# Three chained layers on one core: layer 1's products over token blocks of 512 and 256 instead of 384

## The chip, the cores and the metric

The kernel runs on one core of a Trainium2 chip. The metric is the device time of one execution in microseconds. Time before: median 847.4 us of 3 runs (847.13 to 849.57). TensorE is written PE, VectorE DVE, ScalarE ACT, GpSimd POOL; SP is the engine from whose queue all DMAs are issued.

## The reference

Local attention over q, k, v of shape (4, 8, 576, 64) in chunks of 64 tokens gives 2304 tokens of 512 values. Then two layers with a hidden width of 2048:

```python
x = attention(q, k, v)              # (2304, 512), softmax inside chunks of 64
h = x @ w_in1                       # layer 1, up
x = (h * tanh(log1p(exp(h)))) @ w_out1   # layer 1, down
h = x @ w_in2                       # layer 2, up
g = where(h >= 1, h, where(h <= -1, 0, (h + 1) ** 2 / 4))
out = g @ w_out2                    # layer 2, down, (2304, 512) float32
```

The weights arrive as 64-bit floats, two 32-bit words each.

## The kernel before, in words

Every matrix product is done in three passes of a reduced-precision float format (fp32r): an operand is split into a high and a low half, and high x high, high x low and low x high are added up in PSUM. The weights are loaded as words, put together into 32-bit floats by ACT, POOL and DVE, and split (w_part: the high half is `hi`, a copy on ACT or DVE, the low half `lo` at L345, a subtraction on POOL or DVE).

Stage 1 is attention, 18 tiles of 128 tokens, and layer 1's up product. attention() loads q, k, v, transposes on PE (L505), makes scores (L521), exponentiates on ACT (L542), normalises, transposes again (L565), multiplies with v (L577) and writes the two halves of its part of x (the second at L592). Three tiles fill one x block of 384 tokens; two x blocks are in memory at a time. up() multiplies one x block with one of 16 slices of w_in1: 12 matmuls of 384 columns into one of four banks of the set B (L606), called a step here. ACT applies Mish from the bank into a z buffer (L853); two steps share a buffer of 384 KB, and z_store sends it to DRAM (L616). There are two such buffers. Attention uses the four banks of the set A.

Stage 2 is layer 1's down product. g_pair loads 384 KB of z back (L631), ACT makes the high half and DVE the low half (L636); down() adds 12 matmuls of 384 columns of each slice into four banks (L653), one per 128 output columns, over 16 slices. The blocks alternate between the bank sets A and B. At a block's end the banks are copied (ACT or DVE) and stored to DRAM (L873).

Stage 3, layer 2's up product, multiplies sevenfold: seven products of smaller matrices take the place of eight, so x and the weights are first added and subtracted. x_seven loads one of three groups of 768 tokens (L441), makes sums with DVE (L386) and splits them (L380 and a copy), into seven pieces `x2` per group. w_seven does the same to the weights and stores them to DRAM (L406); w_back loads them (L409). seven() does one unit: one group with one weight slice, 42 matmuls of 384 columns (L780), in four banks of A or B in turn. Stage 4, layer 2's down product, works likewise with 256 columns (L723).

The order of instructions on each engine is set ahead by a planner (class Plan). Each operation has an engine, an assumed duration, a due time (prio) and perhaps an earliest time (release); the planner lets time run and picks, on each engine, the ready operation with the least due time. The chip then works through each engine's fixed list, waiting with semaphores. Buffers without a ring have fixed places in one memory of 154 KB per partition (PLACES); an operation on one waits until everything that lay there has been read. Fixed rings are listed in FIXED: "z" has two places of 3072 bytes, "z2" six.

Before the first up product, PE is given filler matmuls (L942) in its idle time; they end with the second up step.

Of the kernel before, what the change touches and what calls it, by code (L numbers as in the profile page):

```python
# [8 lines left out]
F32 = mybir.dt.float32  # L9
F32R = mybir.dt.float32r  # L10
# [154 lines left out]
def kernel(  # L165
# [28 lines left out]
    NBLK = NT // NB  # L194
    scale = 1.0 / float(D) ** 0.5
# [8 lines left out]
    spill = [dp.tile([P, 2 * NB], F32, name=f"z{b}") for b in range(NBLK * NF // 2)]  # L204
# [3 lines left out]
    x2d = [dp.tile([P, KD * NB], F32, name=f"x{b}") for b in range(NBLK)]  # L208
# [225 lines left out]
    def x_seven(q, tau, after=()):  # L434
# [3 lines left out]
        for d, t in ((0, 0), (0, 1), (1, 1), (1, 0)):  # L438
            x = xs[d, t] = ("xh", q, d, t)
            new(x, "ld" if q == 2 else "z" if d == 0 else "z2", [P, 2, NB])  # L440
            dma(384, lambda _, x=x, d=d, t=t: nc.sync.dma_start(  # L441
                out=get(x).rearrange("p m t -> p (m t)"), in_=x2d[2 * q + t][:, 2 * d * NB:2 * (d + 1) * NB]
            ), reads=[("x2d", 2 * q + t, m) for m in (2 * d, 2 * d + 1)] + list(after), writes=[x], tiles=[x], prio=tau)
# [32 lines left out]
    def attention(i, tau, release=0.0):  # L476
# [81 lines left out]
        op(*(("DVE", 0.69) if i < TB else (("DVE", "POOL"), (0.69, 1.6))), norm, reads=[("ri", i)], writes=[e], tiles=[e], **kw)  # L558
# [26 lines left out]
        x, o = ("x", i // TB), i % TB * P  # L585
        if o == 0:
            new(x, None, [P, 2, KD, NB], F32R)
# [9 lines left out]
    def up(n, x, b, j, xkeys, tau, tag):  # L597
        h, w = ("h", n, b, j), ("w", n, j)
        new(h, tag, [P, 512])

        def products(_):
            wt, xt, ps = get(w), get(x), get(h)[:, 0:NB]
# [8 lines left out]
        op("PE", 2.09, products, reads=[*xkeys, (w, 0), (w, 1)], writes=[h], tiles=[h, w, x], prio=tau)  # L611
        return h

    def z_store(n, b, jp, tau):
        z = ("z", n, b, jp)
        dma(384, lambda _: nc.sync.dma_start(  # L616
            out=spill[b * NF // 2 + jp].rearrange("p (j t) -> p j t", j=2) if n == 0 else
            spill2[jp].rearrange("p (j t) -> p j t", j=2)[:, :, b * NB:(b + 1) * NB], in_=get(z)
        ), reads=[(z, 0), (z, 1)], writes=[("spill", n, b, jp)], tiles=[z], prio=tau)

    pairs = []

    def g_pair(b, jp, tau):

        zl, g = ("zl", b, jp), ("g", 0, b, jp)
        new(zl, "z2", [P, 2, NB])
        new(g, None, [P, 2, 2, NB], F32R)

        after = pairs[-3:-2]
        pairs.append((g, 0))  # L630
        dma(384, lambda _: nc.sync.dma_start(  # L631
            out=get(zl).rearrange("p j t -> p (j t)"), in_=spill[b * NF // 2 + jp]
        ), reads=[("spill", 0, b, jp), *after], writes=[zl], tiles=[zl], prio=tau, release=tau - 20)
        op("ACT", 0.86, lambda e: copy(e, get(g)[:, 0], get(zl)),
           reads=[zl], writes=[(g, 0)], tiles=[zl, g], prio=tau)
        op("DVE", 0.98, lambda _: nc.vector.tensor_tensor(  # L636
# [3 lines left out]
    def down(b, j, tau):  # L640
        w, g, a = ("w", 1, j), ("g", 0, b, j // 2), j % 2
# [5 lines left out]
        def products(_):  # L647
            wt, gt = get(w), get(g)
            gh, gl = gt[:, 0, a], gt[:, 1, a]
            for m, y in enumerate(ys):  # L650
                wh, wl = (wt[:, x, m * P:(m + 1) * P] for x in range(2))
                for x, (l, r) in enumerate(((wh, gh), (wh, gl), (wl, gh))):
                    nc.tensor.matmul(  # L653
                        out=get(y)[:, 0:NB], lhsT=l, rhs=r, start=(j == 0 and x == 0), stop=(j == NF - 1 and x == 2)
# [320 lines left out]
```

## Time and profile before

| | |
|---|---|
| median of the runs | 847.4 us |
| span of the profiled execution | 846.0 us (the runs lie 1.1 to 3.6 us above it) |
| PE busy | 833.0 us, 98% |
| DVE, ACT, POOL busy | 613.1, 422.9, 94.8 us |
| first up step, first down step, first step of layer 2 | 37.09, 279.57, 479.25 us |
| DMA | 205.55 MB, mean 243 GB/s |

Times in rows are microseconds from the span's start. Matmuls are pipelined: a row's duration runs to the modelled end of its last matmul, so the pace is read from starts.

### The profile page before, as it was taken

The numbers are of one execution on the slowest core, as the hardware profiler recorded it, in microseconds if no ns is written. First come the engines' busy times: TensorE is split into PE (matmuls) and PEld (weight loads), VectorE is DVE, ScalarE is ACT, GpSimd is POOL, SyncE is SP. The second block draws the span as 40 slices with busy tenths as digits, with TensorE's granted clock in tenths as the row PEclk, the third lists the DMA queues.
The fourth block names the chain that finished last, engine by engine and source line by source line (L and its number), as shares of the span: only waits on it lengthen the run. The fifth ranks groups of instructions, "written<-read, shape, count | busy, mean of one in ns | idle before, by whom it ended". The sixth has DMA issues, their size and how long they took to land.

```text
span 846.0 us, 16274 instructions
## 1 busy us (share of the span) xinstructions
PE 833.0 (98%) x6358; PEld 817.8 (97%) x6358; DVE 613.1 (72%) x1062; ACT 422.9 (50%) x656; POOL 94.8 (11%) x104
## 2 busy tenths in 40 slices
PE   9999999999999999999999999999999899999997
PEld 8899999999999999999999999999999899999997
DVE  4898867587735768588657788666777679878883
ACT  3574646566634434355434566555566434333341
POOL 1464212133301010000000000000000000000000
PEclk9999999999999999999999999999999999999999
DMA  8869675899779989988898936655679965444431
GB/s 197 212 207 266 193 212 163 247 279 276 210 246 363 327 317 353 364 330 279 308 362 300 355 150 214 243 193 194 239 247 405 401 216 161 127 136 134 142 101 50
DMA packets 145581, 205.55 MB, mean 243 GB/s; under 512 B 63840, under 2 KB 114016, under 8 KB 141408
## 3 DMA queue, kind: packets, MB, share of 16 engines
q1 hardware_dynamic: 145504, 204.51, 72.1%
q8 instruction: 50, 0.82, 0.4%
q14 instruction: 27, 0.22, 0.1%
HBM read 123.73 MB, written 80.74 MB: 242 GB/s over the span
## 4 chain that ended last, share of the span: by engine, by line
PE 86%; DMA 7%; DVE 4%; ACT 2%; issue 1%; POOL 0%; SPq 0%; DVEq 0%; ACTq 0%; POOLq 0%
PE B L606 18%; PE A L653 12%; PE B L653 12%; PE A L723 11%; PE A L780 10%; PE B L723 10%; PE B L780 9%; DMA memory<-in_moe_w_in_dram 3%; PE A L505 2%; PE B L942 2%; DMA zz<-memory 1%; DMA memory_r<-v 1%; PE A L521 1%; PE A L577 1%; DMA memory<-in_moe_w_out_dram 1%
## 5 line engine op out<-in xcount | busy, mean ns | idle before, releaser
L275 ACT ACTIVATE memory_r<-memory 128x768 fp32r<-128x768 f32 (+3 forms) x206 | 163.6, 827 | 204.9 <-PE A L653 28.8
L606 PE MATMUL B<-memory_r 128*128 128x384 f32 x1152 | 213.8, 339 | 1.1 <-POOL memory_r L345 0.8
L606 PEld LDWEIGHTS B<-memory_r 128*128 128x128 f32 x1152 | 197.6, 188 | 4.2 <-POOL memory_r L345 1.3
L723 PE MATMUL A<-memory_r 128*128 128x256 f32 x840 | 104.0, 283 | 2.1 <-DVE memory_r L699 1.1
L723 PEld LDWEIGHTS A<-memory_r 128*128 128x128 f32 x840 | 102.1, 192 | 2.9 <-DVE memory_r L699 1.6
L653 PE MATMUL A<-memory_r 128*128 128x384 f32 x576 | 101.6, 334 | 0.0
L653 PE MATMUL B<-memory_r 128*128 128x384 f32 x576 | 101.6, 334 | 0.0
L653 PEld LDWEIGHTS A<-memory_r 128*128 128x128 f32 x576 | 100.0, 188 | 0.0
L653 PEld LDWEIGHTS B<-memory_r 128*128 128x128 f32 x576 | 100.0, 188 | 0.0
L780 PE MATMUL A<-memory_r 128*128 128x384 f32 x504 | 91.6, 335 | 1.3 <-ACT memory L275 0.7
L780 PE MATMUL B<-memory_r 128*128 128x384 f32 x504 | 90.7, 334 | 0.0
L780 PEld LDWEIGHTS A<-memory_r 128*128 128x128 f32 x504 | 87.5, 188 | 2.8 <-ACT memory L275 1.4
L699 DVE TENSOR_TENSOR memory_r<-memory,memory_r 128x768 fp32r<-128x768 f32 (+1 forms) x72 | 76.9, 1087 | 15.6 <-ACT memory_r L275 15.0
L780 PEld LDWEIGHTS B<-memory_r 128*128 128x128 f32 x504 | 87.5, 188 | 0.2 <-DMA memory_r<-v 0.2
L723 PE MATMUL B<-memory_r 128*128 128x256 f32 x672 | 82.8, 283 | 0.0
L316 POOL TENSOR_SCALAR memory<-memory 128x512 f32<-128x512 f32 x64 | 49.5, 775 | 290.2 <-ACT memory L313 288.0
L723 PEld LDWEIGHTS B<-memory_r 128*128 128x128 f32 x672 | 81.6, 192 | 0.0
L636 DVE TENSOR_TENSOR memory_r<-memory,memory_r 128x768 fp32r<-128x768 f32 x48 | 46.0, 962 | 45.9 <-ACT memory_r L275 42.8
L853 ACT ACTIVATE memory<-B 128x384 f32<-128x384 f32 x96 | 44.9, 489 | 47.9 <-PE B L606 38.2
L380 DVE TENSOR_TENSOR memory_r<-memory,memory_r 128x768 fp32r<-128x768 f32 (+3 forms) x69 | 56.2, 829 | 8.2 <-ACT memory_r L275 8.0
L685 DVE TENSOR_TENSOR memory<-memory 128x256 f32<-128x256 f32 (+1 forms) x108 | 52.3, 508 | 7.7 <-DMA memory<-zz 6.8
L275 ACT ACTIVATE memory<-A 128x512 f32<-128x512 f32 (+2 forms) x58 | 30.5, 541 | 50.4 <-PE A L505 21.1
(54 smaller groups left out, 812.6 us busy)
## 6 DMA issues: line engine op xcount, KB each, us to landing
z<-memory SPq DMA_DIRECT2D x48, 384.0 KB, 3.6
memory<-z SPq DMA_DIRECT2D x48, 384.0 KB, 6.3
zz<-memory SPq DMA_DIRECT2D x48, 384.0 KB, 4.2
memory<-zz SPq DMA_DIRECT2D x72, 256.0 KB, 3.3
memory<-in_moe_w_in_dram SPq DMA_DIRECT2D x32, 512.0 KB, 5.5
memory<-in_moe_w_out_dram SPq DMA_DIRECT2D x32, 512.0 KB, 6.3
v<-memory_r SPq DMA_DIRECT2D x16, 1024.0 KB, 7.9
memory_r<-v SPq DMA_DIRECT2D x16, 1024.0 KB, 9.2
```

The costliest lines, as they stand in the source:

```text
L275: nc.scalar.activation(out=out, in_=in_, func=AF.Copy)
L316: nc.gpsimd.tensor_scalar(out=get(dec), in0=get(dec), scalar1=HIGH, scalar2=-HIGH, op0=ALU.min, op1=ALU.max)
L380: nc.vector.tensor_tensor(out=out(1), in0=in_(), in1=out(0).bitcast(F32), op=ALU.subtract)
L505: nc.tensor.transpose(out=get(ps)[:, p, :], in_=get(qk)[:, x, 2 * p:2 * p + 2, :].rearrange("t h d -> t (h d)"), identity=ident,)
L606: nc.tensor.matmul(out=ps, lhsT=a, rhs=xt[:, r, kk, :], start=(kk == 0 and y == 0), stop=(kk == KD - 1 and y == 2),)
L636: op("DVE", 0.98, lambda _: nc.vector.tensor_tensor(out=get(g)[:, 1], in0=get(zl), in1=get(g)[:, 0].bitcast(F32), op=ALU.subtract), reads= ...
L653: nc.tensor.matmul(out=get(y)[:, 0:NB], lhsT=l, rhs=r, start=(j == 0 and x == 0), stop=(j == NF - 1 and x == 2))
L685: op("DVE", length, lambda _: nc.vector.tensor_tensor(out=out(), in0=a(), in1=b(), op=ALU.subtract), reads=reads, writes=writes, tiles=[zl ...
L699: op("DVE", length, lambda _, a=a, b=b, x=x, c=c: nc.vector.tensor_tensor(out=get(g)[:, :, 1, a:b], in0=get(x)[:, :, c:], in1=get(g)[:, :, ...
L723: nc.tensor.matmul(out=get(ys[bank])[:, half], lhsT=gt[:, l, c], rhs=wt[:, a, r], start=(jp == 0 and half == 0 and y == 0), stop=(jp == NF ...
L780: nc.tensor.matmul(out=ps, lhsT=l, rhs=xt[:, r, kk, :], start=(first and kk == 0 and y == 0), stop=(kk == 1 and y == 2), skip_group_check= ...
L853: op("ACT", 0.5, lambda _, h=h, z=z, j=j: nc.scalar.activation(out=get(z)[:, j % 2], in_=get(h)[:, 0:NB], func=AF.Mish), reads=[h], writes ...
```

## The change

Layer 1's tokens are cut into blocks of 512, which fill a PSUM bank, and one of 256: for the up product the 256 come first (UP: tiles 0 and 1; then four tiles each), for the down product last (DOWNS). The number of blocks is five instead of six. Mish's result of one step is now one z buffer (512 x 4 bytes per partition), stored by itself into a DRAM tensor per slice; g_load brings one slice of one block instead of two slices. The rings keep their sizes. x blocks now lie at 138 and 122 KB, g at 14 to 38 KB in six places, the last two slices of w_out1 at 38 and 62 KB, the x2 groups one third further on (group 0 at 42 to 84 KB, where slices 0 to 4 and 15 of w_out1 lie), w7s at 122 and 0 KB, and the planner's durations and due times follow the widths. Up's blocks have 4 attention tiles, spaced over the block before. x2d, layer 1's output in DRAM, is one tensor per half.

```diff
+    WIDE = 512
+    UP = [(0, NT % WIDE)] + [(NT % WIDE + i * WIDE, WIDE) for i in range(NT // WIDE)]
+    DOWNS = [(i * WIDE, WIDE) for i in range(NT // WIDE)] + [(NT - NT % WIDE, NT % WIDE)]
+    TILES = [range(t // P, (t + n) // P) for t, n in UP]
+    OF = {i: b for b, r in enumerate(TILES) for i in r}
...
-    ORDER = (4, 1, 0, 3, 5, 6, 2)
+    ORDER = (4, 1, 0, 2, 5, 6, 3)
...
-        "w": lambda n, j: KB * ((4 * j, 66 + 4 * j if j < 15 else 60)[n]),
-        "x": lambda b: KB * (130 + 12 * (b % 2)),
-        "g": lambda n, b, jp: KB * (42 + 6 * ((b * NF // 2 + jp) % 3)),
-        "g7": lambda u: KB * (28, 126, 140)[u % 3],
-        "x2": lambda q, c: KB * (42 * q + 6 * ORDER[c]),
+        "w": lambda n, j: KB * ((4 * j, (66 + 4 * j) if j < 14 else (38, 62)[j - 14])[n]),
+        "x": lambda b: KB * (138 - 16 * (b % 2)),
+        "g": lambda n, b, j: KB * (14 + 4 * ((b * NF + j) % 6)),
+        "g7": lambda u: KB * (70, 126, 140)[u % 3],
+        "x2": lambda q, c: KB * (42 * ((q + 1) % 3) + 6 * ORDER[c]),
         "w7": lambda n, jp: KB * (126 + 14 * (jp % 2)),
-        "w7s": lambda n, jp: KB * (126, 140)[n - 2],
-        "wb": lambda jp: KB * (14, 0, 70, 56, 42, 112, 98, 84)[jp],
+        "w7s": lambda n, jp: KB * (122, 0)[n - 2],
+        "wb": lambda jp: KB * (56, 42, 112, 98, 84, 28, 14, 0)[jp],
...
+    def g_load(b, j, tau):
+        (start, width), zl, g = DOWNS[b], ("zl", b, j), ("g", 0, b, j)
+        new(zl, "z2", [P, width])
+        new(g, None, [P, 2, width], F32R)
+        after = made[-5:-4]
+        made.append((g, 0))
+        dma(width / 2, lambda _: nc.sync.dma_start(out=get(zl), in_=spill[j][:, start:start + width]),
+            reads=[*(("spill", 0, u, j) for u in over(start, width, UP)), *after], writes=[zl], tiles=[zl], prio=tau, release=tau - 20)
...
+    long = lambda width: 12 * (width / 2400 + 0.0134)
     t1 = 33.0
-    step = 2.62
-    due = lambda b, j: t1 + step * (b * NF + j)
+    begin = [t1 + sum(NF * (long(n) + 0.0014 * n) for _, n in UP[:b]) for b in range(len(UP) + 1)]
+    due = lambda b, j: begin[b] + j * (long(UP[b][1]) + 0.0014 * UP[b][1])
     for i in range(NT // P):
-        b = i // TB
-        if b < 2:
+        b = OF[i]
+        if i < 6:
             attention(i, 3.0 * i)
         else:
-            attention(i, due(b - 1, 0) + 11 * (i % TB) - 12, release=due(b - 1, 0) + 11 * (i % TB) - 14)
+            t = begin[b - 1] + (begin[b] - begin[b - 1]) * (i - TILES[b][0]) / len(TILES[b]) - 12
+            attention(i, t, release=t - 2)
...
     for bp in range(NBLK // 2):
         x_seven(bp, (t2 + 140, t3 - 12, t3 + 2)[bp], after=[
-            ("step", 0, *((2, 0), (NBLK - 1, 10), (NBLK - 1, NF - 1))[bp]), *(before if bp == 2 else []),
+            ("step", 0, *((2, 0), (len(DOWNS) - 1, 10), (len(DOWNS) - 1, NF - 1))[bp]), *(before if bp == 2 else []),
         ])
```

## Rows read from the trace of the kernel before

**Rows 1.** The page: engine, busy us, share of the span, instructions.
```profile
PE 833.0 (98%) x6358; PEld 817.8 (97%) x6358; DVE 613.1 (72%) x1062; ACT 422.9 (50%) x656; POOL 94.8 (11%) x104
```

**Rows 2.** Timeline of PE, down product: start, duration, line, operation, count.
```profile
279.57 29.28 PE L653 MATMUL A<-memory_r 128*128 128x384 f32 x168
308.69 2.24 PE L653 MATMUL B<-memory_r 128*128 128x384 f32 x12
```

**Rows 3.** Timeline of PE, layer 2's down product.
```profile
667.22 2.68 PE L723 MATMUL B<-memory_r 128*128 128x256 f32 x21
669.74 2.44 PE L723 MATMUL A<-memory_r 128*128 128x256 f32 x19
```

**Rows 4.** Timeline of PE, first up steps; in brackets idle time before, and releaser.
```profile
37.09 2.33 PE L606 MATMUL B<-memory_r 128*128 128x384 f32 x12
...
54.20 8.95 PE L606 MATMUL B<-memory_r 128*128 128x384 f32 x50
63.96 6.49 PE L606 MATMUL B<-memory_r 128*128 128x384 f32 x34 [0.81 <-POOL memory_r L345]
```

**Rows 5.** Timelines of DVE and POOL: x of tiles 1 and 5, weight slices 7, 8.
```profile
28.01 0.70 DVE L592 TENSOR_TENSOR memory_r<-A,memory_r 128x256 fp32r<-128x256 f32 x2
51.77 1.09 DVE L345 TENSOR_TENSOR memory_r<-memory,memory_r 128x512 fp32r<-128x512 f32 x1
55.59 0.74 DVE L592 TENSOR_TENSOR memory_r<-A,memory_r 128x256 fp32r<-128x256 f32 x2
...
55.45 1.29 POOL L345 TENSOR_TENSOR memory_r<-memory,memory_r 128x512 fp32r<-128x512 f32 x1
```

**Rows 6.** Busy time by windows: PE, PEld, DVE, ACT, POOL, granted clock, DMA.
```profile
20.00:40.00 20.00, 18.42 (x296) 17.05 (x296) 17.81 (x40) 11.39 (x24) 7.98 (x8) 1.00 0.88 209
40.00:60.00 20.00, 20.00 (x229) 18.89 (x222) 19.86 (x39) 15.75 (x26) 13.14 (x12) 1.00 0.72 228
```

**Rows 7.** Timeline of ACT: the first load of Mish's table.
```profile
40.57 1.28 ACT L853 ACT_TABLE_LOAD   x1
```

**Rows 8.** z stores: the page's issues; landings in 240:280; groups by form, 512-wide copies.
```profile
z<-memory SPq DMA_DIRECT2D x48, 384.0 KB, 3.6
...
DMA to landing us min/median/max: 3.1/5.7/9.5
...
L275 ACT ACTIVATE memory_r<-memory 128x512 fp32r<-128x512 f32 x33 | 20.7, 627 | 21.9 <-DVE memory L336 20.3 <-PE B L606 1.5
```

**Rows 9.** Timelines of SP, DVE, PE: tile 17's last load, its x, the steps after.
```profile
212.25 0.87 SPq L486 DMA_DIRECT2D memory<-in_k_dram  x1
238.05 0.76 DVE L592 TENSOR_TENSOR memory_r<-A,memory_r 128x256 fp32r<-128x256 f32 x2
237.48 42.25 PE L606 MATMUL B<-memory_r 128*128 128x384 f32 x240
```

**Rows 10.** Timelines of PE and ACT: layer 2's first step, copies of y from B.
```profile
479.25 2.25 PE L780 MATMUL A<-memory_r 128*128 128x384 f32 x12
...
480.03 0.47 ACT L275 ACTIVATE memory<-B 128x384 f32<-128x384 f32 x1
482.61 0.50 ACT L275 ACTIVATE memory<-B 128x384 f32<-128x384 f32 x1
```

**Rows 11.** Windows (columns as rows 6); groups by form: DVE's splits of 768 columns.
```profile
470.00:480.00 10.00, 10.00 (x60) 10.00 (x59) 7.45 (x11) 4.86 (x8) 0.00 (x0) 1.00 0.94 320
...
L380 DVE TENSOR_TENSOR memory_r<-memory,memory_r 128x768 fp32r<-128x768 f32 x21 | 19.7, 952 | 2.6 <-ACT memory_r L275 2.5
```

**Rows 12.** Timeline of SP: loads of layer 2's weights; landing of the load at 472.26.
```profile
472.26 0.38 SPq L409 DMA_DIRECT2D memory_r<-v  x1
483.54 0.38 SPq L409 DMA_DIRECT2D memory_r<-v  x1
...
DMA to landing us min/median/max: 7.8/7.8/7.8
```

More of the change, by code (lines that the diff above doesn't have):

```diff
@@ L194 @@
     NBLK = NT // NB
+    WIDE = 512
[3 more added lines that the diff above has]
+    OF = {i: b for b, r in enumerate(TILES) for i in r}
+    over = lambda t, n, blocks: [b for b, (u, m) in enumerate(blocks) if u < t + n and t < u + m]
     scale = 1.0 / float(D) ** 0.5
@@ L203 @@
     half = const.tile([P, 1], F32, name="half")
-    spill = [dp.tile([P, 2 * NB], F32, name=f"z{b}") for b in range(NBLK * NF // 2)]
+    spill = [dp.tile([P, NT], F32, name=f"z{j}") for j in range(NF)]
     spill2 = [dp.tile([P, 2 * NT], F32, name=f"zz{j}") for j in range(NF // 2)]
@@ L207 @@
     wd_seven = [[dp.tile([P, 7 * 4 * P], F32, name=f"v{n}_{j}") for j in range(NF // 2)] for n in range(2)]
-    x2d = [dp.tile([P, KD * NB], F32, name=f"x{b}") for b in range(NBLK)]
+    x2d = [dp.tile([P, 2 * NT], F32, name=f"x{d}") for d in range(2)]
     FIXED = {
@@ L441, in x_seven @@
             dma(384, lambda _, x=x, d=d, t=t: nc.sync.dma_start(
-                out=get(x).rearrange("p m t -> p (m t)"), in_=x2d[2 * q + t][:, 2 * d * NB:2 * (d + 1) * NB]
-            ), reads=[("x2d", 2 * q + t, m) for m in (2 * d, 2 * d + 1)] + list(after), writes=[x], tiles=[x], prio=tau)
+                out=get(x), in_=x2d[d].rearrange("p (m t) -> p m t", m=2)[:, :, (2 * q + t) * NB:(2 * q + t + 1) * NB]
+            ), reads=[("x2d", b, m) for b in over((2 * q + t) * NB, NB, DOWNS) for m in (2 * d, 2 * d + 1)] + list(after),
+                writes=[x], tiles=[x], prio=tau)
         def put(c, x):
@@ L609, in products, with z_store @@
                     )
-        op("PE", 2.09, products, reads=[*xkeys, (w, 0), (w, 1)], writes=[h], tiles=[h, w, x], prio=tau)
+        op("PE", long(width), products, reads=[*xkeys, (w, 0), (w, 1)], writes=[h], tiles=[h, w, x], prio=tau)
         return h
-    def z_store(n, b, jp, tau):
-        z = ("z", n, b, jp)
+    def z_store(b, jp, tau):
+        z = ("z", 1, b, jp)
         dma(384, lambda _: nc.sync.dma_start(
[L617 to L634, printed above, removed]
+            out=spill2[jp].rearrange("p (j t) -> p j t", j=2)[:, :, b * NB:(b + 1) * NB], in_=get(z)
+        ), reads=[(z, 0), (z, 1)], writes=[("spill", 1, b, jp)], tiles=[z], prio=tau)
+    made = []
+    def g_load(b, j, tau):
[6 more added lines that the diff above has]
+            reads=[*(("spill", 0, u, j) for u in over(start, width, UP)), *after], writes=[zl], tiles=[zl], prio=tau, release=tau - 20)
+        op("ACT", 0.22 + width / 1220, lambda e: copy(e, get(g)[:, 0], get(zl)),
            reads=[zl], writes=[(g, 0)], tiles=[zl, g], prio=tau)
-        op("DVE", 0.98, lambda _: nc.vector.tensor_tensor(
+        op("DVE", 0.15 + width / 930, lambda _: nc.vector.tensor_tensor(
             out=get(g)[:, 1], in0=get(zl), in1=get(g)[:, 0].bitcast(F32), op=ALU.subtract
@@ L653, in products @@
                     nc.tensor.matmul(
-                        out=get(y)[:, 0:NB], lhsT=l, rhs=r, start=(j == 0 and x == 0), stop=(j == NF - 1 and x == 2)
+                        out=get(y)[:, 0:width], lhsT=l, rhs=r, start=(j == 0 and x == 0), stop=(j == NF - 1 and x == 2)
                     )
-        op("PE", 2.09, products, reads=[(g, x) for x in range(2)] + [(w, 0), (w, 1)],
+        op("PE", long(width), products, reads=[(g, x) for x in range(2)] + [(w, 0), (w, 1)],
            writes=[*ys, ("step", 0, b, j), *([("yend", b)] if j == NF - 1 else [])], tiles=[w, g, *ys], prio=tau)
@@ L858 @@
     for j in range(NF):
         w_part(1, j, t1 + 60 + 10 * j, release=t1 + 40 + 8 * j)
-    t2 = due(NBLK, 0)
-    due2 = lambda b, j: t2 + 2.09 * (b * NF + j)
-    for b in range(NBLK):
+    t2 = begin[-1]
+    begin2 = [t2 + sum(NF * long(n) for _, n in DOWNS[:b]) for b in range(len(DOWNS) + 1)]
+    due2 = lambda b, j: begin2[b] + j * long(DOWNS[b][1])
+    for b, (start, width) in enumerate(DOWNS):
         for j in range(NF):
             tau = due2(b, j)
-            if j % 2 == 0:
-                g_pair(b, j // 2, tau - 24)
+            g_load(b, j, tau - 24)
```

49 lines of the change are left out of this document (26 added, 23 removed).

## The prediction

> **What bounds the kernel now.** I read the busy shares first: TensorE (PE) is busy for 98% of the span, VectorE (DVE) for 72% [rows 1]. Matmuls overlap, so a busy share proves little, and I turned to starts. In the down product 168 matmuls of 384 columns start within 308.69 - 279.57 = 29.12 us, 173.3 ns each, with no gap [rows 2]. In layer 2, 21 matmuls of 256 columns take 669.74 - 667.22 = 2.52 us, 120.0 ns each [rows 3]. The two points give columns at 2.4 GHz (160.0 and 106.7 ns) plus 13.3 ns per matmul. From 37.09 us on PE runs at this rate nearly without a break; its first product waits until then for the weights and for the first x block [rows 4, 5]. So the end moves by what PE has to execute after about 37 us, plus the waits put into its line.
>
> **The change, part by part.**
>
> Fewer matmuls. Each product has 192 passes over the tokens (16 slices of 12 matmuls). Before: 192 x 6 x 173.3 = 199.7 us. After, with 512 columns at 213.3 + 13.3 = 226.7 ns: 192 x (4 x 226.7 + 120.0) = 197.1 us. Two products: 384 matmuls fewer, -5.1 us, all on the path, since PE is the bound in both stages. No row has 512 columns; the ends are 213.3 ns (columns alone, -25.6 us in all) and 240 ns (two of 256, +15.4 us). I take 226.7, on the line through both rows.
> The Trainium skill (TensorE: Matmul & The Clock Gate, Back-to-back issue gap) gives a warm gap of N/2.4 + 2.5 ns. By it 384 matmuls would be worth only 384 x 2.5 = 1.0 us and the sum below would be 4.1 us higher; the rows show 13.3 ns here, so the measurement decides.
>
> The start. Now the first x block holds two attention tiles instead of three. Tile 1's second half is written at 28.01 + 0.70 = 28.71 us, tile 5's at 55.59 + 0.74 = 56.33 [rows 5]. Up steps may begin at about 29 instead of 37 us. But each one needs its weight slice, and slices come in slowly: the seventh's low half is finished at 51.77 + 1.09 = 52.86 us, the eighth's at 55.45 + 1.29 = 56.74 [rows 5]. Both come from a DVE that is busy 17.81 to 19.86 us of 20 [rows 6], and the change takes nothing off it there. Before, PE ran the six steps from 37.09 us on and the seventh from 54.20 to 54.20 + 2.08 = 56.28 [rows 4]: 7 x 2.08 = 14.6 us of work. After, the same seven slices allow seven steps of 256, 7 x 1.44 = 10.1 us. The next block (tiles 2 to 5) can't start before 56.3 us, as tile 5 couldn't earlier. So 4.5 us of the work are pushed behind 56 us. Against it stands the wait of 0.81 us for a weight's low half [rows 4]: behind 56 us eight slices lie ready for the 512 block, 21.8 us of work, so that wait has cover (-1.0 with its restart). Net +3.5 us; ends 0 (tile 5 comes 4 us sooner because shorter steps stand before its matmuls) and +7.
>
> Table loads. ScalarE's mish and exp sit in different tables, 1.28 us per load [rows 7]. The first mish comes at 31 instead of 40.57 us, among the exps of tiles 3 to 5: one to two pairs of loads more, and tile 5 may slip by 1.3 to 2.6 us. PE then executes the eighth step of block 0 (1.44 us), which is due anyway, so I take 0, with +2 as the far end.
>
> The z stores. Two slots held two steps each, now one step each. A slot's turn is mish 0.6 (a copy of 512 takes 627 ns [rows 8]), issue 0.4, landing, hops 0.2. At the median landing of 3.6 us [rows 8] this is 4.8 us for one slot, 2.4 us per step with two, under the 2.72 us of a step. Toward the end of the stage landings are 5.7 in the median and 9.5 at worst [rows 8], 3.4 to 5.3 us per step: ScalarE then stands behind a store, and with it the g copies and weight conversions queued on it. The four B banks let PE run 4 x 2.72 = 10.9 us ahead, and walking the last block store by store with the old landings, the lag reaches some 5 us. Cost 0; ends 0 and +6. A gain is excluded: no store stopped PE before. SP gets 32 more z stores and 32 more z loads of about 0.4 us each, spread over 400 us; and 2 KB packets for 3 KB. Taken as nothing, because loads run 10 steps ahead; the cover gone, each late load would cost its lateness.
>
> Attention's lead. The last tile of a block was released 33.9 planner's microseconds before the next block (16 x 2.62 - 8), now 16 x 3.44 x 1/4 + 14 = 27.8. Tile 17's load went out at 212.25 us and its x was written at 238.81, 26.6 us later [rows 9]. Twenty steps were left at 237.48 us, four of them of its predecessor, so it led by 7 us. With 6.1 us less the lead is 1 us. Three block starts are concerned: +0.5, ends 0 and +5. The tiles' wider spacing speaks for less.
>
> The down product. No gap before [rows 2]; 80 conversions of g on ScalarE and DVE take the place of 48 longer ones, beside idle time. With blocks alternating between bank sets A and B, the fifth block ends in A, where layer 2's first unit also begins; before, the sixth ended in B. So that unit now waits for the copies of y. Before, the stage ended at 479.25 us and ScalarE copied y between x2 copies from 480.03 to 482.61 + 0.50 [rows 10]: the first bank came free after 1.2 us, the last after 3.9. Product 0 needs one bank, the next follow at 1.04 us each: +1.2, ends 0.6 (a copy at once) and 3.9.
>
> The x2 pieces. Layer 2's first x pieces used to lie where layer 1's first weights had been, free since the up stage. Now four of seven lie over slices 0 to 4 and 15 of the down weights, in use until the last block, whose steps run 23 us. A chain of 11 DVE instructions of 0.952 us = 10.5 us [rows 11] moves from the middle of the down stage to its last 20 us. There DVE was busy 7.45 of 10 us [rows 11], idle some 5 in 20, and g subtractions rise by 2. Some 7 us don't fit and push back the second group of x pieces. Before, the unit that reads it ran second in layer 2, because the second weight slice was loaded only at 483.54 us, behind a store in its place [rows 12]; that place is free earlier now, so the group can be wanted 7.3 us later. Ends 0 and +7; I take +1.
>
> Layer 2's first weights. The second part of the first slice went out at 472.26 us and took 7.8 us: it landed at 480.05, 0.8 us after the down stage's end at 479.25 [rows 10, 12]. Its timetable hangs on the down stage's begin, not its end, and the stage is 2.6 us shorter: it is 3.4 us late now, for a second product that starts 1.0 + 1.2 us in. +0.5 (half of the 1.2 us, since the bank wait and the x chain hide the rest); ends 0 and +2.6.
>
> Sum: -5.1 + 3.5 + 0.5 + 1.2 + 1 + 0.5 = +1.6 us on a span of 846.0. The median of the runs is 847.4, 1.4 above the span, which I keep: 849.0 us. What a measurement of this kernel can tell from no change is 0.3%, 2.5 us: 844.9 to 849.9 counts as the same.
>
> **The rivals.**
> Faster: the start costs nothing, because tile 5 comes sooner, and layer 2's entry only its bank wait: -5.1 + 1.2 = -3.9, 843.5 us; anything better than -2.5 belongs here. For it speaks that matmuls are the one bound seen everywhere; against it the full DVE before 56 us [rows 6].
> Slower at the entry of layer 2: the x chains don't fit and PE waits for the second group. Place: the start of layer 2's first unit that reads it. It decides from about 4 us of lateness on: -5.1 + 3.5 + 0.5 + 1.2 + 4.5 + 0.5 = +5.1, 852.5 us. For it: DVE's little idle time [rows 11]; against: eleven instructions can go between others.
> Slower in the up stage: the two z slots, or a late x block, stop PE. It decides when ScalarE's lag passes the 10.9 us of four banks, or the lead falls under zero: +5 on the sum, 854.0 us. For it: landings of 9.5 us [rows 8]; against: before, none of these landings stopped PE.
> The clock: the filler matmuls before the first product now end at about 31 us, not 40, and then PE has only seven short steps (10.1 us) and the attention of three tiles in some 25 us. The granted clock was 1.00 there [rows 6], so no row shows it at the lower level. If it fell to 1.2 GHz and block 1 began so, its first step would take 2.56 us longer, twelve times 213.3 ns of columns once more: 851.6 us.
> The Trainium skill (TensorE: Matmul & The Clock Gate, What's actually happening) says that the default state is throttled and activity releases it; that speaks for this rival.
> No gain at all from wide matmuls (240 ns): 849.0 + 5.1 + 15.4 = 869.5 us; only the straight line speaks against it.
>
> **How the numbers follow.** The forecast 0.38, the faster rival 0.27, layer 2's entry 0.19, the up stage 0.10, the clock 0.04, dear wide matmuls 0.02. So faster 0.27, same 0.38, slower 0.35. The range runs from 843 (the faster rival and half a microsecond) to 855 (the up-stage rival and some of the entry); about 0.2 lies outside. Within the forecast alone: 846 to 850.
>
> **What would show it.** Matmuls of 512 starting 226.7 ns apart in the down stage, and that stage 197.1 us long (step 1). First up matmul at about 29 us, gaps on PE between 31 and 56 us, block 1 beginning near 56 to 58 us (the start). The first down matmul within 1.5 us of 280 us: the up stage loses what it gains. A wait of about 1 us on PE for an A bank at the first layer-2 product, with ACT or DVE as releaser. ScalarE idle behind z stores but PE not. The prediction is wrong if PE is stopped in the up stage by B banks, if layer 2 begins under 476 us, or if layer 2's first three units wait for DVE by more than 3 us.

## The result, and the profile after

The changed kernel takes 859.99 us (median of 4 runs, 858.35 to 860.43) beside 848.49 us for the kernel before (4 runs, 847.13 to 850.1): ratio 1.0141, 95% interval 1.0117 to 1.0164. It is slower by 11.5 us; 849.0 was forecast, and the range ended at 855. The profiled spans are 857.9 and 846.0 us, +11.9.

In the changed kernel's code the up matmuls are L615, the down ones L660, layer 2's up L787 and down L730; layer 2's x pieces are loaded at L447, its weights at L415; g's low half is L643, the x pieces' low half L386, their sums L392, the additions of layer 2's units L805, Mish L861, copies L281.

The page's busy shares (to set beside [rows 1]): 418 matmuls fewer, and 1.3 us less of busy time, in a span 11.9 us longer. Idle time on PE has come in.

```profile
PE 831.7 (97%) x5940; PEld 755.0 (88%) x5940; DVE 610.2 (71%) x1095; ACT 428.6 (50%) x670; POOL 92.2 (11%) x103
```

Timeline of PE in the down product of the kernel after (start, duration, line, operation, count; answers to [rows 2]): 84 matmuls of 512 columns start within 320.02 - 300.98 = 19.04 us, 226.7 ns each.

```profile
300.98 19.20 PE L660 MATMUL A<-memory_r 128*128 128x512 f32 x84
320.02 2.88 PE L660 MATMUL B<-memory_r 128*128 128x512 f32 x12
```

Timeline of PE at the start (answers to [rows 4]). The first step is at 30.67 us, but by 56.3 us only 74 matmuls of 256 columns have begun: 74 x 0.120 = 8.9 us of up work where the kernel before had 14.6. Behind the steps stand waits for attention and for weights. Tile 5's x, the gate of the second block, was written at 57.05 + 0.74 = 57.79 us. The last line is PE's longest wait between 60 and 460 us, for a bank that Mish still reads.

```profile
30.67 1.68 PE L615 MATMUL B<-memory_r 128*128 128x256 f32 x12
...
45.01 1.11 PE L572 MATMUL A<-ident,memory 128*128 128x128 f32 x4 [2.81 <-POOL memory L563]
...
47.97 4.54 PE L615 MATMUL B<-memory_r 128*128 128x256 f32 x24
...
56.57 1.69 PE L615 MATMUL B<-memory_r 128*128 128x256 f32 x12 [1.22 <-POOL memory_r L351]
...
88.25 3.02 PE L615 MATMUL B<-memory_r 128*128 128x512 f32 x12 [0.82 <-ACT memory L861]
```

Seven down steps (19.0 us) now run between the last up steps, and the pure down stretch begins at 300.98 us; without them the up product would have ended at 281.9, against 279.57 [rows 2]. That is 2.4 us later although 2.56 us of matmuls are saved: the start cost 4.9 us.

Timeline of PE at the entry of layer 2 (answers to [rows 10]). Two things are to be seen. Layer 2's products (L787) stand among the last down steps from 460.33 us on, 42 of them, one whole unit, before the end of the last down step at 492.4. Before, the first came when down was done [rows 10]. And at 511.28 and 515.88 PE has stood still for a ScalarE copy and a VectorE addition.

```profile
460.33 1.21 PE L787 MATMUL B<-memory_r 128*128 128x384 f32 x6
461.38 1.59 PE L660 MATMUL A<-memory_r 128*128 128x256 f32 x12
...
474.84 1.70 PE L660 MATMUL A<-memory_r 128*128 128x256 f32 x12 [0.51 <-DVE memory_r L643]
...
488.67 0.44 PE L787 MATMUL B<-memory_r 128*128 128x384 f32 x1 [1.39 <-ACT memory_r L281]
...
490.67 1.90 PE L660 MATMUL A<-memory_r 128*128 128x256 f32 x12
492.41 1.26 PE L787 MATMUL B<-memory_r 128*128 128x384 f32 x6
...
511.28 1.32 PE L787 MATMUL A<-memory_r 128*128 128x384 f32 x6 [1.09 <-ACT memory L281]
515.88 5.78 PE L787 MATMUL A<-memory_r 128*128 128x384 f32 x24 [3.29 <-DVE memory L805]
521.50 3.28 PE L787 MATMUL B<-memory_r 128*128 128x384 f32 x18
```

The window of busy time (columns as in [rows 6]; first the kernel after, then the kernel before) shows VectorE nearly full there, the DMA engines at a share of 0.35, and the granted clock below 1. But VectorE had 17.95 of 20 us in the kernel before too, where PE didn't wait: its load alone is not the difference.

```profile
500.00:520.00 20.00, 15.61 (x80) 14.73 (x79) 18.99 (x29) 11.98 (x20) 0.00 (x0) 0.91 0.35 119
```

```profile
500.00:520.00 20.00, 20.00 (x117) 20.00 (x116) 17.95 (x30) 12.16 (x21) 0.00 (x0) 1.00 0.29 96
```

To size it, I took every product matmul's distance to the next start, less its nominal one (columns at 2.4 GHz + 13.3 ns): 13.3 us are lost between 460 and 520 us, against 2.6 us before (480 to 540), +10.7. Between 660 and 680 it is 4.4 against 2.9. Sum: -5.1 + 4.9 + 10.7 + 1.5 = +12.0 for a measured +11.9.

Timeline of SP (issues; answers to [rows 12]). Layer 2's first weights go out at 440.51 us, before at 465.17 and 472.26; the second group's pieces of x from 478.98 us on (before from 458.06); the third group's last at 499.6 to 500.3, behind the stores of the last down block.

```profile
440.51 1.92 SPq L415 DMA_DIRECT2D memory_r<-v  x2
...
478.98 2.02 SPq L447 DMA_DIRECT2D memory<-x  x2
...
493.71 4.24 SPq L882 DMA_DIRECT2D x<-memory  x4
499.59 1.23 SPq L447 DMA_DIRECT2D memory<-x  x2
```

### The profile page after: what moved, and what is told of

Its sections match the earlier page's. It is cut to its first block, busy times and chain, and to the rows that moved or that the text cites. A ratio compares the mean times of both kernels' runs of the same rounds, so it can differ in the third digit from the quotient of the medians.

```text
span 857.9 us, 15675 instructions
## 1 busy us (share of the span) xinstructions
PE 831.7 (97%) x5940; PEld 755.0 (88%) x5940; DVE 610.2 (71%) x1095; ACT 428.6 (50%) x670; POOL 92.2 (11%) x103
## 5 line engine op out<-in xcount | busy, mean ns | idle before, releaser
L281 ACT ACTIVATE memory_r<-memory 128x512 fp32r<-128x512 f32 (+3 forms) x237 | 167.6, 742 | 209.5 <-PE A L660 43.4
L615 PE MATMUL B<-memory_r 128*128 128x512 f32 (+1 forms) x960 | 210.8, 375 | 2.4 <-POOL memory_r L351 1.2
L615 PEld LDWEIGHTS B<-memory_r 128*128 128x128 f32 x960 | 167.1, 191 | 33.4 <-POOL memory_r L351 1.4
L660 PE MATMUL A<-memory_r 128*128 128x512 f32 (+1 forms) x576 | 114.3, 354 | 1.2 <-DVE memory_r L643 1.1
L660 PEld LDWEIGHTS A<-memory_r 128*128 128x128 f32 x576 | 96.0, 189 | 17.1 <-DVE memory_r L643 2.0
L730 PE MATMUL A<-memory_r 128*128 128x256 f32 x840 | 105.3, 285 | 2.1 <-DVE memory_r L706 1.1
L730 PEld LDWEIGHTS A<-memory_r 128*128 128x128 f32 x840 | 103.4, 194 | 2.9 <-DVE memory_r L706 1.5
L787 PE MATMUL A<-memory_r 128*128 128x384 f32 x504 | 92.3, 338 | 4.5 <-DVE memory L805 3.3
L787 PE MATMUL B<-memory_r 128*128 128x384 f32 x504 | 92.7, 336 | 2.8 <-ACT memory_r L281 1.4
L787 PEld LDWEIGHTS A<-memory_r 128*128 128x128 f32 x504 | 88.8, 190 | 5.7 <-DVE memory L805 3.9
L787 PEld LDWEIGHTS B<-memory_r 128*128 128x128 f32 x504 | 87.2, 188 | 4.2 <-DVE memory_r L386 2.6
L643 DVE TENSOR_TENSOR memory_r<-memory,memory_r 128x512 fp32r<-128x512 f32 (+1 forms) x80 | 50.1, 636 | 55.6 <-ACT memory_r L281 49.8
L660 PE MATMUL B<-memory_r 128*128 128x512 f32 x384 | 88.7, 389 | 0.0
L660 PEld LDWEIGHTS B<-memory_r 128*128 128x128 f32 x384 | 72.1, 188 | 15.0
L730 PE MATMUL B<-memory_r 128*128 128x256 f32 x672 | 82.9, 283 | 0.0
L730 PEld LDWEIGHTS B<-memory_r 128*128 128x128 f32 x672 | 81.9, 193 | 0.0
L322 POOL TENSOR_SCALAR memory<-memory 128x512 f32<-128x512 f32 x64 | 47.1, 738 | 304.3 <-ACT memory L319 304.1
L386 DVE TENSOR_TENSOR memory_r<-memory,memory_r 128x768 fp32r<-128x768 f32 (+3 forms) x69 | 56.5, 829 | 13.4 <-ACT memory_r L281 12.2
L281 ACT ACTIVATE memory<-A 128x512 f32<-128x512 f32 (+2 forms) x62 | 32.5, 545 | 61.4 <-PE A L512 25.3
L861 ACT ACTIVATE memory<-B 128x512 f32<-128x512 f32 (+1 forms) x80 | 42.9, 553 | 26.0 <-PE B L615 15.7
```

Of the source, the lines that this page charges most:

```text
L281: nc.scalar.activation(out=out, in_=in_, func=AF.Copy)
L322: nc.gpsimd.tensor_scalar(out=get(dec), in0=get(dec), scalar1=HIGH, scalar2=-HIGH, op0=ALU.min, op1=ALU.max)
L386: nc.vector.tensor_tensor(out=out(1), in0=in_(), in1=out(0).bitcast(F32), op=ALU.subtract)
L615: nc.tensor.matmul(out=ps, lhsT=a, rhs=xt[:, r, kk, :], start=(kk == 0 and y == 0), stop=(kk == KD - 1 and y == 2),)
L643: op("DVE", 0.15 + width / 930, lambda _: nc.vector.tensor_tensor(out=get(g)[:, 1], in0=get(zl), in1=get(g)[:, 0].bitcast(F32), op=ALU.sub ...
L660: nc.tensor.matmul(out=get(y)[:, 0:width], lhsT=l, rhs=r, start=(j == 0 and x == 0), stop=(j == NF - 1 and x == 2))
```

## The experiments

Each was timed beside the kernel before; ratios are to it, with 95% intervals. Three edits recur. **Old places**: ORDER, x2, g7, wb and w7s's second place as before the change, g in four places at 42 KB, the last two slices of w_out1 at 58 and 62 KB (the cut shows parts of the lines). **Up 384s**: the up blocks are 384, 384, 512, 512, 512. **Down 384s**: the down blocks are 512, 512, 512, 384, 384.

```diff
# old places
-    ORDER = (4, 1, 0, 2, 5, 6, 3)
+    ORDER = (4, 1, 0, 3, 5, 6, 2)
-  (66 + 4 * j) if j < 14 else (38, 62)[j - 14]
+  (66 + 4 * j) if j < 14 else (58, 62)[j - 14]
-  "g": KB * (14 + 4 * ((b * NF + j) % 6))
+  "g": KB * (42 + 4 * ((b * NF + j) % 4))
-  "x2": KB * (42 * ((q + 1) % 3) + 6 * ORDER[c])
+  "x2": KB * (42 * q + 6 * ORDER[c])
-  "w7s": KB * (122, 0)[n - 2]
+  "w7s": KB * (122, 140)[n - 2]
...
# up 384s
+    UP = [(0, NB), (NB, NB)] + [(2 * NB + i * WIDE, WIDE) for i in range(3)]
# down 384s
+    DOWNS = [(i * WIDE, WIDE) for i in range(3)] + [(3 * WIDE, NB), (3 * WIDE + NB, NB)]
```

### The start

**Up blocks 384, 512, 512, 512, 384** (the first block as long as before the change).

> The changed kernel with the up product over blocks of 384, 512, 512, 512, 384: as many matmuls, but three attention tiles in the first block again. If the short first block costs the 4.9 us at the start, the up stage ends 4 to 5 us earlier and the time is about 855 us. If the time was lost to the weights or to table loads whatever the first block's width, or layer 2's entry takes it back: 859 to 861 us.

867.97 us, 1.0231 (1.0216 to 1.0247): worse. By 56 us it had the kernel before's 14.6 us of work, but the second block then needs seven tiles, and PE starves from 60 to 100 us. It also stood 5.5 us, in three waits from 331 to 340 us, behind Mish's banks. So one block of 384 in front only moves the hole.

**Fillers until the eighth up step.** In the kernel after, the granted clock fell to 0.5 (1.2 GHz) from 44.4 to 51.2 us; it fell within the wait of 2.81 us above, which ends at 45.01.

```diff
-    reads=[idle, ("h", 0, 0, 1)]
+    reads=[idle, ("h", 0, 0, 7)]
```

> The changed kernel (860.0 us) with the filler matmuls kept until the eighth up step of block 0 instead of the second (they hold one of the four B banks until then). In the changed kernel the granted clock is at half for 6.8 us from 44.4 us on. If that clock is a cost of its own: the up stage ends 1 to 3 us earlier and the time is 857 to 859 us. If the weights and the small first block set the start whatever the clock: 859.5 to 861 us.

859.51 us, 1.0126 (1.0103 to 1.0149). The windows of busy time (columns as in [rows 6]) of this run and of the kernel after show the clock back at 1.00 and no gain in time: PE there waits for tiles and weights, not for itself.

```profile
40.00:60.00 20.00, 19.85 (x270) 19.00 (x260) 19.24 (x40) 14.21 (x23) 9.50 (x9) 1.00 0.78 222
```

```profile
40.00:60.00 20.00, 13.80 (x166) 12.19 (x167) 19.42 (x41) 13.98 (x23) 9.44 (x10) 0.83 0.75 221
```

**Up 384s alone.**

> The changed kernel with the up product over blocks of 384, 384, 512, 512, 512: as many matmuls as the change, but the first two blocks, with their attention tiles, as before. (The earlier try with 384, 512, ... had the start of before until 56 us and then stood without x, since its second block needs a seventh tile.) If the small first block costs the 4.9 us at the start, the up stage ends at about 277 us and the time is 855 us. If the start's loss comes from elsewhere: 859 to 861 us.

857.82 us, 1.0111 (1.009 to 1.0133): 15.3 us of work were done by 56.3 us, so the lost work was won back, but 4 us went again at 60 to 75 us, in waits of 0.6 to 1.9 us on Mish's banks. Two z places hold ScalarE there; that returns below.

### Layer 2's entry

**The bank sets of layer 2 exchanged**, so that its first unit doesn't meet the down product's last banks.

```diff
-                new(y, "AB"[tp % 2], [P, 2, 2 * P])
+                new(y, "BA"[tp % 2], [P, 2, 2 * P])
...
-            new(h, "AB"[u % 2], [P, 512])
+            new(h, "BA"[u % 2], [P, 512])
```

> The changed kernel with layer 2's two bank sets exchanged, so that its first unit uses B while the last down block ends in A. If the bank conflict is what sets layer 2's entry: unit 0 comes first again and the time falls by 4 us or more, to 856 us or less. If the late x2 pieces set it: 858.5 to 861 us.

861.88 us, 1.016 (1.0145 to 1.0175): not the banks.

**Old places in the kernel after**, and, the other way, **the change's places in the kernel before** (x and w7s's first place stay there, and g has four places for pairs of slices).

> The changed kernel (860.0 us) with the old places: x2 group 0 at 0 to 42 KB, g at 42 to 58 KB in four places, the last two slices of w_out1 at 58 and 62 KB, g7, wb and w7s's second place as before; wide blocks and everything else stay. If the late places of x2 group 0 cause the loss at layer 2's entry (13.3 us of lost PE time between 460 and 520 us against 2.6 before), that loss falls to about 3 us and the time to about 850 us. If the bank conflict at the last block or the wide blocks' own conversions cause it, the time stays at 858 to 861 us.

> The kernel before (848.5 us) with the change's places alone (x2 group 0 over slices of w_out1, last two slices at 38 and 62 KB, g at 14 KB on, g7, wb, w7s as changed), blocks of 384 kept. If the places cause the loss at layer 2's entry: 856 to 859 us. If the wide blocks or their bank order cause it: 847 to 850 us.

The first gave 858.77 us, 1.0121 (1.0106 to 1.0137), the second 854.03 us, 1.007 (1.0044 to 1.0096). The places cost 5.7 us where the rest is old, and their return wins 1.2 us where the rest is new. That isn't a sum of two parts.

**The second group's x pieces loaded sooner** (with old places), and the same with up 384s.

```diff
-        x_seven(bp, (t2 + 140, t3 - 12, t3 + 2)[bp], after=[
-    ("step", 0, *((2, 0), (len(DOWNS) - 1, 10), ...
+        x_seven(bp, (t2 + 140, t3 - 30, t3 + 2)[bp], after=[
+    ("step", 0, *((2, 0), (len(DOWNS) - 2, 12), ...
```

> The kernel with the old places (858.8 us) in which the second group of x pieces is put into the order earlier: its loads come after step 12 of the fourth down block instead of step 10 of the short last one. In the kernel before these loads went out 21 us before layer 2 began, in the old-places kernel 9 us before or less, behind stores on SP's queue. If this late place on the queue causes what is left of the loss at layer 2's entry (8.7 us against 2.6): 853 to 855 us. If the DMA engines, full from 460 to 500 us, or VectorE's total work cause it: 858 to 860 us.

> All three: old places, second x group sooner, up blocks of 384, 384, 512, 512, 512. If the start and layer 2's entry are the two losses and add up: 846 to 850 us, and under 848 if the 5.1 us of saved matmuls come through. If layer 2's entry is set by the work that VectorE and the DMAs have to do after the up stage, an earlier end of the up stage is lost again there: 853 us or more.

862.53 us, 1.0172 (1.0137 to 1.0207), and 858.62 us, 1.0118 (1.0097 to 1.0138). The entry after the last down step loses less, but between 460 us and that step's end 13.3 and 12.6 us are lost instead: its steps of 1.44 us run through ten prefetched g slices in 14 us (an estimate from the edits; before: twelve in 25), and the loads now stand behind x pieces and layer 2's weights on SP's queue, as its timeline shows. Timeline of PE, second run:

```profile
484.14 5.60 PE L660 MATMUL A<-memory_r 128*128 128x256 f32 x24 [5.33 <-ACT memory_r L281]
```

**Wide up alone** (old places, up 384s, down 6 x 384) and **both products with 384s** (old places, up 384s, down 384s).

> As the one of six blocks of 384, with the up product alone over 384, 384, 512, 512, 512. 192 matmuls fewer: if the path after the up stage simply follows, 2.6 us less than that one. If layer 2's entry hangs on work that starts at the up stage's end and lasts as long as before, also 2.6 us less; if the z buffers of one step hold PE up, the same or more.

> Up over 384, 384, 512, 512, 512 and down over 512, 512, 512, 384, 384, old places: all the matmuls that the change saves, without a block of 256. If the short last down block (256 columns, 1.44 us a step, its loads landing late while the DMA engines are full) causes what the old places did not give back: 847 to 851 us. If the length of the down stage against layer 2's preparations causes it: 855 us or more.

The first gave 858.36 us, 1.0108 (1.0071 to 1.0145). It has the old places and no block of 256, and still loses 6.4 us between 460 and 520 us: 12 of layer 2's matmuls stand ahead of the last down one there, and its timeline has the wait for an addition.

```profile
516.08 6.72 PE L787 MATMUL A<-memory_r 128*128 128x384 f32 x24 [3.47 <-DVE memory L805]
```

The second gave **848.4 us, 0.999 (0.9966 to 1.0014)**: here the loss at the entry is gone (1.9 us). The next three take this kernel apart again: old places and up 384s with the short last down block; up and down 384s with the change's places; the change with down 384s alone.

> Places of the kernel before, up blocks 384, 384, 512, 512, 512, and the down product still 512, 512, 512, 512, 256: the same as the run that came out at 848.4 us, but for the two down blocks of 384 at the end. Theory S (the short last down block, with steps of 1.44 us, piles the conversions of its intermediate and of layer 2's inputs up at the entry): 855 to 858 us, with 6 to 9 us of lost TensorE time between 460 and 520 us. Rival P (the moved weight slices do it, by holding loads back): 848 to 850 us, since the places are the old ones. Rival X (the earlier loads of the run with everything together did the harm there): 848 to 850 us as well, and its 858.6 us was due to them.

> The change's own places, with up blocks 384, 384, 512, 512, 512 and down blocks 512, 512, 512, 384, 384. Theory S: 848 to 850 us, no loss at layer 2's entry over 3 us. Rival P: 853 to 855 us (the moved places alone cost the kernel before 5.8 us), with 5 us or more lost between 460 and 520 us. If both add, this one is at 853 to 855 and the one with the old places and the block of 256 at 855 to 858.

> The change with one thing altered: the down product's blocks are 512, 512, 512, 384, 384; the first up block stays 256 and the places stay the change's. Theory S: 850 to 853 us (860.0 less the 8 to 10 us lost at the entry). Rival P: 857 to 860 us. The start is as in the change (8.9 us of up work done by 56 us).

| places | up's first | down's last | us | ratio | L787 before the last L660 | unit 4 to 5 |
|---|---|---|---|---|---|---|
| old | 384, 384 | 384, 384 | 848.4 | 0.999 (0.9966 to 1.0014) | 0 | 8.71 |
| old | 384, 384 | 256 | 854.82 | 1.0081 (1.0055 to 1.0106) | 0 | 9.61 |
| new | 384, 384 | 384, 384 | 859.2 | 1.0136 (1.0113 to 1.016) | 48 | 13.67 |
| new | 384, 384 | 256 | 857.82 | 1.0111 (1.009 to 1.0133) | 42 | 13.81 |
| new | 256 | 384, 384 | 860.58 | 1.0157 (1.0134 to 1.018) | 36 | 15.39 |
| new | 256 | 256 (the change) | 859.99 | 1.0141 (1.0117 to 1.0164) | 42 | 13.57 |

The last columns come from PE's timelines: layer 2's matmuls that start before the last down one, and the time from the fourth unit's start to the fifth's (42 matmuls, 7.28 us undisturbed, as in the kernel before). Against the first row the short block alone costs 0.9% and the places alone 1.5%; both together (fourth row) cost no more than the places alone. The table speaks for two mechanisms, which the traces show at work; it doesn't cover the run with wide up alone.

**New places.** The first load of the first unit's weights goes out at 436 to 450 us in every run with these places (old ones: 465 to 480), and in the wide kernels the planner lists the unit among the down steps. Nothing is won: the down product ends a unit later, and what hangs on its end ends later too. Its last block is stored and loaded again as the third group of x, split and added, and read first by the fifth unit. In the four runs of the table with new places, where PE waits at the end of the fourth unit, the fifth begins 27.8 to 31.5 us after the last down matmul. Four units of 7.28 would cover 29.1 us of that, three only 21.8. In the kernel before and in the best run below nothing is ahead and the fourth unit lasts 7.28 us: the fifth begins after 31.1 and 30.3 us without a wait, so there the chain is no longer than that. DRAM is the smaller part of it. In the kernel after the last load of the third group landed at 504.3 us, 12 us after the last down matmul; the other 17 us, until the fifth unit begins at 521.5, went to conversions and additions on VectorE and ScalarE, in their written order.

That the unit ahead is what makes the wait is argued, not shown: no run has these places and holds the unit back. Against a simple rule stand the run with wide up alone (12 matmuls ahead, old places, fourth unit 14.16 us) and the kernel before with the change's places (none ahead, 11.96 us). A rival that no run tests with these places is the second group of x, whose loads go out 21 us later than before. Timelines of PE and DVE in the run with new places and 384s:

```profile
455.65 1.20 PE L787 MATMUL B<-memory_r 128*128 128x384 f32 x6
456.69 2.24 PE L660 MATMUL A<-memory_r 128*128 128x384 f32 x12
...
510.98 6.78 PE L787 MATMUL A<-memory_r 128*128 128x384 f32 x24 [3.66 <-DVE memory L805]
517.59 2.24 PE L787 MATMUL B<-memory_r 128*128 128x384 f32 x12
```

```profile
503.36 0.55 DVE L805 TENSOR_TENSOR memory<-A,memory 128x384 f32<-128x384 f32 x1
503.83 1.82 DVE L386 TENSOR_TENSOR memory_r<-memory,memory_r 128x768 fp32r<-128x768 f32 x2
505.56 0.55 DVE L831 SCALAR_TENSOR_TENSOR memory<-memory 128x384 f32<-128x384 f32 x1
506.03 0.95 DVE L392 TENSOR_TENSOR memory<-memory 128x768 f32<-128x768 f32 x1
506.90 0.95 DVE L386 TENSOR_TENSOR memory_r<-memory,memory_r 128x768 fp32r<-128x768 f32 x1
507.77 0.95 DVE L831 SCALAR_TENSOR_TENSOR memory<-memory 128x768 f32<-128x768 f32 x1
508.64 0.95 DVE L386 TENSOR_TENSOR memory_r<-memory,memory_r 128x768 fp32r<-128x768 f32 x1
509.51 0.95 DVE L392 TENSOR_TENSOR memory<-memory 128x768 f32<-128x768 f32 x1
510.38 0.55 DVE L805 TENSOR_TENSOR memory<-A,memory 128x384 f32<-128x384 f32 x1
```

DVE runs without a pause, and the addition that frees a bank stands behind the third group's conversions. After the wait, the 24 matmuls that start at 510.98 take 6.61 us for 4.16: the granted clock was 0.5 there.

**Short last block, old places.** Here no unit is ahead, but the down product ends sooner (at 477.4, not 480.3 us), and layer 2's weights don't come sooner. Timelines of SP and PE: the first two parts landed at 478.38 and 483.35 us, the second slice, issued at 484.45, at 490.52, each just where PE goes on. With their restarts these three waits are 4.7 us of the 10.2 lost between 460 and 520 us.

```profile
469.50 1.46 SPq L415 DMA_DIRECT2D memory_r<-v  x1
471.58 0.42 SPq L415 DMA_DIRECT2D memory_r<-v  x1
484.45 1.31 SPq L415 DMA_DIRECT2D memory_r<-v  x2
```

```profile
478.52 3.36 PE L787 MATMUL A<-memory_r 128*128 128x384 f32 x18 [0.96 <-DMA memory_r<-v]
483.39 3.60 PE L787 MATMUL A<-memory_r 128*128 128x384 f32 x19 [1.51 <-DMA memory_r<-v]
...
490.57 2.29 PE L787 MATMUL B<-memory_r 128*128 128x384 f32 x6 [1.73 <-DMA memory_r<-v]
```

**The third group due later** (the change, one number altered): if only the written order on DVE held the additions, this would free them.

```diff
-        x_seven(bp, (t2 + 140, t3 - 12, t3 + 2)[bp], after=[
+        x_seven(bp, (t2 + 140, t3 - 12, t3 + 14)[bp], after=[
```

> The change with one number altered: the pieces of x for layer 2's third group are due 12 us later in the planner's list, so that VectorE's list has the units' additions ahead of that group's conversions (three additions in a row where two conversions stood between each). Theory V (VectorE's written order, with 19 of 20 us busy between 500 and 520 us, is what TensorE waits for there): the 6.5 us lost at 500 to 520 go to under 3, and the time is 854 to 857 us. Rival L (the second group's pieces land too late, at 488 to 493 us, whatever the order): 859 to 861 us, with the same 3.5-us wait for an addition.

862.51 us, 1.0157 (1.0133 to 1.0181). Theory V's time wasn't reached, and rival L's wait for an addition is gone: the stretch of 500 to 520 us is without loss, the fifth unit begins only 22 us after the last down matmul, and then PE waits for a converted piece instead, and 7.8 us are lost from 520 us on. The order on VectorE decides where PE waits. The run doesn't show that the chain alone decides how long, for the edit itself lists these conversions later: the last load landed at 507.5 us, and VectorE made the last three low halves only from 524.68 us on.

```profile
517.12 3.46 PE L787 MATMUL A<-memory_r 128*128 128x384 f32 x19
523.95 1.97 PE L787 MATMUL A<-memory_r 128*128 128x384 f32 x5 [3.38 <-DVE memory_r L386]
```

### The z places

The run at 848.4 us still lost 4.5 us at 60 to 102 us. Timeline of PE in it:

```profile
69.12 2.36 PE L615 MATMUL B<-memory_r 128*128 128x384 f32 x12 [0.78 <-ACT memory L861]
72.20 2.36 PE L615 MATMUL B<-memory_r 128*128 128x384 f32 x12 [0.73 <-ACT memory L861]
76.31 2.35 PE L615 MATMUL B<-memory_r 128*128 128x384 f32 x12 [1.75 <-ACT memory L861]
```

**Three z places** (old places, 384s); layer 2's x pieces that used "z" go to "z2".

```diff
-    "z": (2, 3072)
+    "z": (3, 2048)
-    new(x, "ld" if q == 2 else "z" if d == 0 else "z2", [P, 2, NB])
+    new(x, "ld" if q == 2 else "z2", [P, 2, NB])
```

> The run that came out at 848.4 us, with three places of 2048 bytes for Mish's results in place of two of 3072 (layer 2's x pieces that used them go to the six places that the others use). Theory Z (two places, each held over a store's way out, let ScalarE run only one step ahead, so that TensorE waits for the four banks between 60 and 75 us): the waits of 0.9 to 2.0 us there go, and the time is 844 to 846 us. Rival: TensorE waits for ScalarE itself, which is taken up by attention and its table loads there: 848 to 849 us, with the same waits. Second rival: layer 2's x pieces, with two places fewer, come later and cost 1 to 5 us at the entry: 849 to 853 us.

857.48 us, 1.0121 (1.01 to 1.0142). The waits on Mish went, as theory Z said, but the down product lost 16 us: the x pieces took the places of its g loads. Timelines of SP (no g load, L639, between 426.46 and 439.41 us, nor from there to 452.76) and of PE:

```profile
426.46 1.36 SPq L639 DMA_DIRECT2D memory<-z  x2
...
436.68 2.64 SPq L447 DMA_DIRECT2D memory<-x  x2
439.41 1.79 SPq L639 DMA_DIRECT2D memory<-z  x2
...
452.76 4.74 SPq L639 DMA_DIRECT2D memory<-z  x6
```

```profile
451.84 0.44 PE L660 MATMUL A<-memory_r 128*128 128x384 f32 x1 [3.87 <-ACT memory_r L281]
455.86 4.41 PE L660 MATMUL A<-memory_r 128*128 128x384 f32 x14 [3.58 <-DVE memory_r L643]
```

**A third place without that**: every third Mish result lies in an "sh" place.

```diff
-            new(z, "z", [P, width])
+            new(z, "sh" if j % 3 == 2 else "z", [P, width])
```

> The run that came out at 848.4 us, with every third Mish result in one of the four small places that layer 1's up stage leaves nearly unused, in place of one of the two z places; layer 2's pieces of x keep their places, so that the loads of the down product's intermediate are not held as they were in the run with three z places. Theory Z (the two places held TensorE between 60 and 75 us, and the loss in the run with three z places came from the pieces of x that it moved): the waits of 0.8 to 1.9 us on ScalarE's Mish go, the down product has no loss at 420 to 460 us, and the time is 843 to 846 us. Rival: the small places are held by the weight slices' own conversions, and TensorE waits for weights or Mish as before: 847 to 850 us. Second rival: an earlier end of the up product upsets the entry of layer 2 once more: 850 to 858 us.

**843.1 us, 0.993 (0.9906 to 0.9954)**, faster than both kernels; span 841.2 us. PE runs through (its timeline): 94 matmuls without a stop where the waits were, and layer 2 entered without a unit ahead.

```profile
56.51 16.89 PE L615 MATMUL B<-memory_r 128*128 128x384 f32 x94 [0.27 <-POOL memory_r L351]
...
469.73 4.32 PE L660 MATMUL A<-memory_r 128*128 128x384 f32 x24
473.89 2.37 PE L787 MATMUL A<-memory_r 128*128 128x384 f32 x12
```

Two more runs, with up in six blocks of 384 in the new loops (872.93 and 873.34 us), computed another output, and why is open; so their times say nothing, and moving z by single slices was not priced by itself.

## Why the prediction was wrong

- **Fewer matmuls, -5.1: right.** 226.7 ns per 512 columns was measured, the value on the line through [rows 2, 3]; the dear-matmul rival fell with it.
- **The start, +3.5: measured 4.9.** The mechanism held (short steps, slices of weights at the old pace): PE did 8.9 us of work by 56.3 us where 10.1 were allowed for, and tile 5 came at 57.8, not 56.3.
- **Table loads 0, attention's lead +0.5, down product 0:** PE has no wait of more than 0.2 us for attention or for g between 60 and 460 us.
- **The z stores, 0:** nearly right for this kernel: Mish's banks stopped PE once, for 0.82 us. The bound of +6 had substance: with the start repaired, the two places cost 4.5 us.
- **The A-bank wait, +1.2: wrong.** Layer 2's first unit stands in B, among the down steps, and exchanging the sets won nothing.
- **The x2 pieces, +1, and layer 2's first weights, +0.5: the step that failed.** Together with the bank term I had 2.7 us for the entry; 10.7 were measured. I wrote that the second slice's "place is free earlier now, so the group can be wanted 7.3 us later", and treated it as a worry about the second group. The first weights I had 3.4 us late. In truth they went out 25 us earlier, and the planner used it: a whole unit was listed ahead of the last down steps. I had not asked what an earlier weight releases. That the places bring the loss is shown (848.4 against 859.2 us); that they do so through this unit is argued. The price has the place that my rival "slower at the entry of layer 2" named, but falls on the third group, and is longer: the fourth unit lasts 13.57 us instead of 7.28. Of these 6.3 us, 4.7 are the two waits at 511.28 and 515.88 with their restarts, and 1.5 us are the low clock after them (24 matmuls in 5.62 us for 4.16). The rest of the 13.3 us lost between 460 and 520 us, 6.8, lies in the last down block and the unit mixed into it: waits for g, x pieces and a copy at 463 to 490 us.
- **Layer 2's weights against the down product's end**: the mechanism of that term (a timetable that doesn't follow an earlier end) was real, but only with the old places, where three waits of 0.96 to 1.73 us show it.
- **The clock:** it fell at the start, as that rival said, and showed no cost there (fillers: 859.51 against 859.99 us); it cost 1.5 to 2.5 us behind the waits at the entry, where I had not looked. The Trainium skill (TensorE: Matmul & The Clock Gate, What's actually happening) lets activity release the clock; both falls began within a wait of PE, which agrees.

What stays open: which of the place edits brings the weights forward. w7s's second place leaving 140 KB, where the second slice of layer 2's weights lies, fits the times but wasn't tried alone. Open too is why the kernel before with these places (weights at 445.73 us) got no unit ahead and still lost 5.7 us, why wide up alone lost 6.4 us at the entry with the old places, and what the later loads of the second group of x cost.

## What to carry to other kernels

A buffer moved so that something can start sooner also changes what a list scheduler puts there: look at what the earlier data release, and whether the work pulled forward was covering a latency behind it. Where a stage's end feeds a later one through DRAM, measure that chain (here 28 to 31 us from the last down matmul to the fifth unit, 12 of them through DRAM) and ask how much independent work stands behind the end, and not ahead of it. And where two edits each cost, undoing one alone may win next to nothing (here 1.2 us of 11.5): undo both before calling a cause innocent.

## What was not expected of the hardware

The pace of matmuls in this format is the same line at three widths: 120.0, 173.3 and 226.7 ns for 256, 384 and 512 columns, 13.3 ns over the columns at 2.4 GHz. In waits of 3.29 us (the kernel after) and 3.66 us (new places and 384s) at the entry the granted clock fell to 0.5, where it stayed from 515.4 to 518.8 and from 509.2 to 516.0 us. The wait of 3.66 us was followed by 24 matmuls that took 2.45 us more than at full clock: there a wait cost two thirds as much again. At the kernel after's own entry, 1.46 us followed waits of 4.4. With old places and the short last block no wait between 470 and 500 us was longer than 1.73 us, and the clock was 0.5 all the same from 490.5 to 493.9 us, behind four waits within 13 us.
